# Banded attention and a PReLU feed-forward: the slots of the opening rearranged

## The chip, the core and the metric

The kernel runs on one core of a Trainium2 chip. The core has a matrix engine (PE, with its weight loads shown as PEld), a vector engine (DVE), a scalar engine (ACT), a general engine (POOL) and a queue that issues most of the DMAs (SP). Each works through its own instructions in the order in which they are written and waits where an operand is not ready. The metric is device time in microseconds (us); less is better.

## The reference

Inputs are `q`, `k`, `v` of shape (8, 8, 576, 64): batch, heads, positions, head size. Attention is causal with a window of 64 positions; its output, as 4608 tokens of 512 values, goes through a feed-forward layer of width 2048:

```python
rel = pos[:, None] - pos[None, :]
scores = np.where((rel >= 0) & (rel < 64), scale * q @ k.T, -1e9)
attn = softmax(scores);  x = attn @ v            # -> 4608 x 512
h = x @ w_in
g = np.maximum(h, 0) + alpha * np.minimum(h, 0)
out = (g @ w_out).astype(np.float32)
```

The weights come as 64-bit floats. The kernel keeps more precision than one reduced product would give: every operand of the two large products is a high part and a low part, and each product is three (low x high, high x low, high x high).

## The kernel before

**Tiles and blocks.** The 4608 tokens are 36 tiles of 128. They form blocks of 2, 2, 2 and then 3 tiles; `f` counts 16 slices of 128 of the hidden width. One *cell* (n, f) is block n with slice f: the hidden product H (L300, twelve matmuls into a PSUM bank `ph`); the slopes (L309, ACT: bank times a slope, into `g`); the larger (L310, DVE: maximum of the other slope and `g`); the split (L319, ACT, high part `gh`; L320, POOL, low part `gl`); and the output product (L332, three matmuls for each tile, accumulated over all 16 slices in a bank of their own).

**Attention of one tile.** Scores (L209, PE); per head a mask, row minimum and its readout (L223, DVE) and an exponential (L226, ACT); scaling by the reciprocal sum (L232 and L233 on DVE, L234 on POOL); transposes (L247, PE) with a copy (L248, ACT); values (L259, PE); the split of the result into `xh` (L262, ACT) and `xl` (L263, DVE). Its loads are L180, L183 and L191.

**Conversion of the weights.** DMAs bring the 64-bit weights as pairs of 32-bit words, in 32 *chunks*: chunk 2f is slice f of `w_in`, chunk 2f+1 that of `w_out`. A chunk c passes through: fetch (L114, SP); exponent mask `two` (L123, DVE) and its rebias (L125, ACT); mantissa mask `man` (L130, DVE) and its conversion (L133, ACT); the joins `exp` (L140, DVE) and `val` (L142, DVE); the product of both (L148, POOL); the high part (L159, ACT); the low part (L163, POOL), which needs the high part. H(n, f) needs chunk 2f, the output product of (n, f) needs chunk 2f+1.

**The opening.** `opening()` is written out by hand, and each engine runs it in this order. After a prologue with tiles 0 and 1 and chunks 0 to 2 it goes through *slots*, j = 3, 4, and so on. In slot j chunk j is masked, chunk j-1 joined and multiplied, chunk j-2 split. Slots also hold the cells of blocks 0 and 1 and one of five attention steps for tiles 2 to 5 (`STEPS`, slots 3 to 22: load, half the scores and their exponentials; the other half and a scaling; a scaling and half the transposes; the other half; the values). Block 0 has a cell in every second slot from slot 3 on, since a slice takes two chunks. Block 1 joins when tiles 2 and 3 are there, at slot 13; for five slots there are then two cells a slot to catch up, and after that one, of alternating blocks, until slot 34.

The order within a slot before is: H of the cell; high part (j-2); joins (j-1); fetch (j+2); low part (j-2); slopes and larger of the cell; product (j-1); exponent mask and rebias (j); split of the cell; mantissa mask and conversion (j); output product of an earlier cell; a second cell, whole; the attention step.

**Buffers that matter.** `ph` has two PSUM banks, shared by H and `two`; `psa` two, shared by `man`, the scores, the transposes and the values; `raw` holds three chunks; `val` and `exp` two each.

**After the opening** a loop over blocks 2 to 12 alternates cells with eighths of the attention of later tiles. Its instructions stand behind those of the opening on every engine. The diff does not touch it, but for `m_slopes`, cut in two and called one after the other.

Of the kernel before, what the change touches and what calls it, by code (L numbers as in the profile page):

```python
# [8 lines left out]
F32 = mybir.dt.float32  # L9
# [4 lines left out]
ALU = mybir.AluOpType  # L14
# [11 lines left out]
def banded_attention_then_prelu_ffn(  # L26
# [93 lines left out]
    def mask_exp(c):  # L120
        d = cv[c]
        d["two"] = two = ps_h.tile([P, E], I32, tag="ph", name=f"two_{c}")
        nc.vector.tensor_scalar(out=two, in0=d["high"], scalar1=0x7FF00000, scalar2=None,  # L123
                                op0=ALU.bitwise_and)
        nc.scalar.activation(two, two, AF.Relu, scale=8.0, bias=ebias)  # L125

    def mask_man(c):
        d = cv[c]
        d["man"] = man = ps_a.tile([P, E], I32, tag="psa", name=f"man_{c}")
        nc.vector.tensor_scalar(out=man, in0=d["high"], scalar1=0xFFFFF, scalar2=0x100000,  # L130
                                op0=ALU.bitwise_and, op1=ALU.bitwise_or)

        nc.scalar.activation(man.bitcast(F32), man, AF.Copy,  # L133
                             scale=s20_sb[:, c // 2:c // 2 + 1] if c % 2 else 2.0**-20)

    def join(c):
        d = cv[c]
        d["val"] = val = io.tile([P, E], F32, tag="val", name=f"val_{c}", bufs=2)
        d["exp"] = exp = io.tile([P, E], I32, tag="exp", name=f"exp_{c}", bufs=2)
        nc.vector.scalar_tensor_tensor(out=exp, in0=d["high"], scalar=-2**31, in1=d["two"],  # L140
                                       op0=ALU.bitwise_and, op1=ALU.bitwise_or)
        nc.vector.scalar_tensor_tensor(out=val, in0=d["low"],  # L142
                                       scalar=s52_sb[:, c // 2:c // 2 + 1] if c % 2 else 2.0**-52,
                                       in1=d["man"].bitcast(F32), op0=ALU.mult, op1=ALU.add)
# [54 lines left out]
    def a_score(t, halves=(0, 1)):  # L199


        d = st[t]
        q, k = d["q"], d["k"]
        d["s"] = [a_bank(t, f"s_{t}_{u}") for u in halves]
        for e in range(NP):
            for h in range(2):
                for u in halves:
                    r, out_ = slice(u * D, (u + 1) * D), slice(h * W, (h + 1) * W)
                    nc.tensor.matmul(d["s"][u - halves[0]][out_, e], q[r, e, h, :], k[r, e, :, h, :],  # L209
                                     start=True, stop=True)  # L210
# [17 lines left out]
    def a_norm(t, halves=(0, 1)):  # L228
        d = st[t]
        g = slice(halves[0] * NP, (halves[-1] + 1) * NP)  # L230
        w, rc = d["w"][:, g, :], d["rc"][:, g]
        nc.vector.tensor_scalar_add(rc, d["sm"][:, g], 1e-9)  # L232
        nc.vector.reciprocal(rc, rc)  # L233
        nc.gpsimd.tensor_tensor(out=w, in0=w, in1=rc.unsqueeze(2).broadcast_to(list(w.shape)),  # L234
                                op=ALU.mult)
# [69 lines left out]
    def m_slopes(n, f):  # L305
        nt = len(blocks[n]) * P
        ph = gs[n, f]
        g = gp.tile([P, nt], F32, tag="g", name=f"g_{n}_{f}", bufs=2)
        nc.scalar.activation(g, ph[:, :nt], AF.Copy, scale=sa_sb[:, f:f + 1])  # L309
        nc.vector.scalar_tensor_tensor(out=g, in0=ph[:, :nt], scalar=s_sb[:, f:f + 1], in1=g,  # L310
                                       op0=ALU.mult, op1=ALU.max)
        gs[n, f] = g

    def m_split(n, f):
        nt = len(blocks[n]) * P
        g = gs[n, f]
        gh = gp.tile([P, nt], F32R, tag="gh", name=f"gh_{n}_{f}")
        gl = gp.tile([P, nt], F32R, tag="gl", name=f"gl_{n}_{f}")
        nc.scalar.copy(gh, g)  # L319
        nc.gpsimd.tensor_tensor(out=gl, in0=g, in1=gh.bitcast(F32), op=ALU.subtract)  # L320
        gs[n, f] = gh, gl
# [27 lines left out]
    def cell(n, f):  # L349
        m_hidden(n, f)  # L350
        m_slopes(n, f)
        m_split(n, f)
        late.append((n, f))
        while len(late) > LAG:
            m_out(*late.pop(0))
# [3 lines left out]
    def soft(t, u):  # L359
        for e in range(NP):  # L360
            a_soft(t, u * NP + e)
# [15 lines left out]
    def opening():  # L377
        a_load(0)
        fetch(0)
        nc.scalar.dma_start(alpha_sb, alpha.rearrange("(f p) -> p f", p=P))  # L380
        a_load(1)
        v_load(0)
        fetch(1)
        v_load(1)
        fetch(2)
        a_score(0)
        soft(0, 0)
        soft(0, 1)
        mask_exp(0)
        mask_man(0)  # L390
        a_norm(0)
        nc.vector.tensor_scalar(out=s_sb, in0=alpha_sb, scalar1=1.0, scalar2=-2.0, op0=ALU.is_gt, op1=ALU.mult)
        nc.vector.tensor_scalar_add(s_sb, s_sb, 1.0)
        nc.vector.tensor_scalar_mul(s20_sb, s_sb, 2.0**-20)
        nc.vector.tensor_scalar_mul(s52_sb, s_sb, 2.0**-52)
        nc.vector.tensor_tensor(out=sa_sb, in0=s_sb, in1=alpha_sb, op=ALU.mult)
        join(0)
        fetch(3)
        product(0)
        a_score(1)  # L400
        a_transpose_pe(0, 0)
        a_transpose_pe(0, 1)
        high_part(0)
        soft(1, 0)
        soft(1, 1)
        a_value(0)
        low_part(0)
        mask_exp(1)
        mask_man(1)
        a_norm(1)  # L410
        load(2)
        join(1)
        fetch(4)
        product(1)
        mask_exp(2)
        mask_man(2)
        a_transpose_pe(1, 0)
        a_transpose_pe(1, 1)
        high_part(1)
        low_part(1)  # L420
        a_value(1)

        done, wait = [0, 0], []
        first = [0, 5 * sizes[1]]
        j = LEAD
        while done != [NF, NF] or wait:

            ready = [n for n in range(2) if j - LEAD >= first[n]]
            at = min(NF, (j - LEAD) // 2 + 1)
            behind = sum(at - done[n] for n in ready)  # L430
            cells = []
            for _ in range(min(behind, 2 if behind > 2 else 1)):
                n = min(ready, key=lambda n: done[n])
                cells.append((n, done[n]))
                done[n] += 1
            if cells:
                m_hidden(*cells[0])
            if 0 <= j - 2 < 2 * NF:
                high_part(j - 2)
            if j - 1 < 2 * NF:  # L440
                join(j - 1)
            fetch(j + 2)
            if j - 2 < 2 * NF:
                low_part(j - 2)
            if cells:
                m_slopes(*cells[0])
            if j - 1 < 2 * NF:
                product(j - 1)
            if j < 2 * NF:
                mask_exp(j)  # L450
            if cells:
                m_split(*cells[0])
            if j < 2 * NF:
                mask_man(j)
            if wait and 2 * wait[0][1] + 1 + LEAD <= j:
                m_out(*wait.pop(0))
            for c in cells[1:]:
                m_hidden(*c)
                m_slopes(*c)
                m_split(*c)  # L460
                if wait and 2 * wait[0][1] + 1 + LEAD <= j:
                    m_out(*wait.pop(0))
            wait += cells
            while len(wait) > 2:
                m_out(*wait.pop(0))
            t, k = divmod(j - LEAD, 5)
            if t + 2 < EARLY:
                STEPS[k](t + 2)
            j += 1
# [60 lines left out]
```

## Time and profile before

| | |
|---|---|
| time, median of 3 runs | 979.17 us (977.67 to 979.46) |
| profiled execution | 978.52 us, its span 976.8 us |
| PE busy | 927.3 us, 95% of the span |
| DVE busy | 464.1 us, 48% |
| ACT busy | 422.4 us, 43% |
| POOL busy | 350.9 us, 36% |
| chain that ended last | PE 86%, ACT 6%, DVE 3% |

Shares are of the whole span, and the opening is its first 183 us or so. Of the groups that only the opening has (conversion), POOL's product (32 of 1.285 us) and low part (33 of about 1.28 us) are the longest instructions. A row of the timeline gives the start, the length, the engine, the line, the operation, result and operands, and in brackets the idle time before it and what ended that.

### The profile page before, as it was taken

The page shows a single profiled execution, that of the slowest core. Times are in us where ns is not written, and L with a number is a line of the kernel's source. Part 1 is how long each engine was busy: PE and PEld are TensorE (multiplying, and loading weights), DVE is VectorE, ACT ScalarE, POOL GpSimd, SP SyncE. Part 2 cuts the span into 40 slices and gives each one's busy share as a digit, 9 for nine tenths or more (in the row PEclk, how much of TensorE's full clock was granted, in tenths as well). Part 3 has the DMA queues.
Part 4 walks back from the last instruction along what each step waited for, and adds up shares of the span by engine and source line. Part 5 has one row for each costly group of instructions (what it writes and reads, how often), then busy time and mean ns, then how long its engine had stood idle before and what let it go on. Part 6 is the DMA issues. An engine that isn't in the chain of part 4 may idle for free.

```text
span 976.8 us, 17281 instructions
## 1 busy us (share of the span) xinstructions
PE 927.3 (95%) x6576; PEld 814.7 (83%) x6576; DVE 464.1 (48%) x1394; ACT 422.4 (43%) x1174; POOL 350.9 (36%) x327
## 2 busy tenths in 40 slices
PE   3677988999999999999999999999999999999998
PEld 3556867888888888888888888889889889889997
DVE  4675678475444444444544454444444444441111
ACT  4565666644433442442443443433433433432322
POOL 3575689433223223223223322322232223222221
PEclk9879999999999999999999999999999999999999
DMA  9865384332321321321322322322322322100000
GB/s 212 176 164 140 98 197 138 106 79 59 89 66 30 98 61 36 90 66 41 87 61 48 87 55 55 87 55 54 87 56 54 87 56 55 55 1 1 33 1 33
DMA packets 96419, 74.54 MB, mean 76 GB/s; under 512 B 44624, under 2 KB 89680, under 8 KB 96336
## 3 DMA queue, kind: packets, MB, share of 16 engines
q1 hardware_dynamic: 94272, 73.42, 30.0%
q8 instruction: 52, 0.85, 0.4%
q10 hardware_dynamic: 2064, 0.01, 0.1%
q14 instruction: 31, 0.25, 0.1%
HBM read 63.97 MB, written 9.44 MB: 75 GB/s over the span
## 4 chain that ended last, share of the span: by engine, by line
PE 86%; ACT 6%; DVE 3%; issue 2%; DMA 1%; SPq 1%; POOL 1%; POOLq 0%; ACTq 0%
PE h L300 40%; PE o L332 38%; PE av L259 4%; PE s L209 4%; DVE two L123 1%; ACT two L125 1%; ACT w L226 1%; ACT g L309 1%; PE t L247 1%; ACT man L133 1%; SPq L183 1%; DMA q<-qT 1%; DMA v<-vN 1%; DVE pt L242 1%; ACT gh L319 1%
## 5 line engine op out<-in xcount | busy, mean ns | idle before, releaser
L320 POOL TENSOR_TENSOR gl<-g,gh 128x384 fp32r<-128x384 f32 (+1 forms) x208 | 197.2, 948 | 471.5 <-ACT gh L319 369.8
L310 DVE SCALAR_TENSOR_TENSOR g<-h,s_sb,g 128x384 f32<-128x384 f32 (+1 forms) x208 | 122.1, 587 | 301.8 <-ACT g L309 299.2
L332 PE MATMUL o<-wout_h,gl 128*128 128x512 f32 x576 | 227.9, 396 | 13.9 <-POOL gl L320 13.9
L332 PE MATMUL o<-wout_l,gh 128*128 128x512 f32 x576 | 228.4, 397 | 0.0
L332 PE MATMUL o<-wout_h,gh 128*128 128x512 f32 x576 | 226.0, 392 | 0.0
L309 ACT ACTIVATE g<-h,sa_sb 128x384 f32<-128x384 f32 (+1 forms) x208 | 115.6, 556 | 254.1 <-PE h L300 253.7
L300 PE MATMUL h<-xh,win_l 128*128 128x384 f32 (+1 forms) x832 | 180.7, 339 | 11.1 <-POOL win_l L163 5.9
L319 ACT CAST gh<-g 128x384 fp32r<-128x384 f32 (+1 forms) x208 | 101.1, 486 | 188.7 <-DVE g L310 188.6
L242 DVE STREAM_TRANSPOSE pt<-w 32x256 f32<-32x256 f32 x360 | 157.0, 436 | 53.5 <-POOL w L234 48.3
L300 PE MATMUL h<-xl,win_h 128*128 128x384 f32 (+1 forms) x832 | 170.3, 326 | 0.0
L300 PEld LDWEIGHTS h<-xh,win_l 128*128 128x128 f32 x832 | 139.3, 190 | 36.0 <-DVE g L310 8.4
L300 PE MATMUL h<-xh,win_h 128*128 128x384 f32 (+1 forms) x832 | 169.0, 324 | 0.0
L300 PEld LDWEIGHTS h<-xl,win_h 128*128 128x128 f32 x832 | 143.5, 190 | 0.3 <-DVE xl L263 0.2
L300 PEld LDWEIGHTS h<-xh,win_h 128*128 128x128 f32 x832 | 140.9, 190 | 0.0
L226 ACT ACTIVATE w<-w,nm 128x128 f32<-128x128 f32 x288 | 112.2, 392 | 54.7 <-DVE nm L223 54.7
L332 PEld LDWEIGHTS o<-wout_h,gl 128*128 128x128 f32 x576 | 108.8, 189 | 31.7 <-POOL gl L320 15.2
L332 PEld LDWEIGHTS o<-wout_h,gh 128*128 128x128 f32 x576 | 109.1, 189 | 24.3
L332 PEld LDWEIGHTS o<-wout_l,gh 128*128 128x128 f32 x576 | 109.2, 190 | 14.4
L234 POOL TENSOR_TENSOR w<-w,rc 128x1024 f32<-128x1024 f32 (+1 forms) x40 | 69.0, 1726 | 120.1 <-DVE rc L233 99.0
L223 DVE CUSTOM_DVE_ANT_0 w<-s,masks 128x128 f32<-128x128 f32 x288 | 64.2, 286 | 64.6 <-PE s L209 64.5
L209 PE MATMUL s<-k,q 64*64 64x128 f32 x1152 | 50.1, 287 | 12.0 <-DMA q<-qT 10.7
L209 PEld LDWEIGHTS s<-k,q 64*64 64x64 f32 x1152 | 38.9, 139 | 26.9 <-DMA k<-kT 11.8
(43 smaller groups left out, 509.8 us busy)
## 6 DMA issues: line engine op xcount, KB each, us to landing
k<-kT SPq DMA_DIRECT2D x72, 256.0 KB, 4.0
v<-vN SPq DMA_DIRECT2D x72, 256.0 KB, 4.2
q<-qT SPq DMA_DIRECT2D x144, 64.0 KB, 3.6
out<-os SPq DMA_DIRECT2D x36, 256.0 KB, 2.4
raw<-w_in SPq DMA_DIRECT2D x16, 512.0 KB, 4.3
raw<-w_out SPq DMA_DIRECT2D x16, 512.0 KB, 3.5
alpha_sb<-alpha ACTq DMA_DIRECT2D x1, 8.0 KB, 4.6
```

What stands on the lines that cost most here:

```text
L209: nc.tensor.matmul(d["s"][u - halves[0]][out_, e], q[r, e, h, :], k[r, e, :, h, :], start=True, stop=True)
L223: nc.vector.tensor_tensor_reduce(out=w, in0=d["s"][u % len(d["s"])][:, e], in1=mask, op0=ALU.add, op1=ALU.min, scale=-SCALE, scalar=3.0e38 ...
L226: nc.scalar.activation(w, w, AF.Exp, scale=-1.0, bias=nm, accum_out=d["sm"][:, g:g + 1])
L234: nc.gpsimd.tensor_tensor(out=w, in0=w, in1=rc.unsqueeze(2).broadcast_to(list(w.shape)), op=ALU.mult)
L242: nc.vector.transpose(pt[ks, :, r], w[r, :, ks])
L259: nc.tensor.matmul(av[r, e, u * W:(u + 1) * W], v[:, e, u, r], pt[:, u * NP + e, h * W:(h + 1) * W], start=True, stop=True)
L300: nc.tensor.matmul(ph[:, :nt], wt[:, c, fs], xt[:, c, xs], start=(k == 0), stop=(k == 3 * NP - 1))
L309: nc.scalar.activation(g, ph[:, :nt], AF.Copy, scale=sa_sb[:, f:f + 1])
L310: nc.vector.scalar_tensor_tensor(out=g, in0=ph[:, :nt], scalar=s_sb[:, f:f + 1], in1=g, op0=ALU.mult, op1=ALU.max)
L319: nc.scalar.copy(gh, g)
L320: nc.gpsimd.tensor_tensor(out=gl, in0=g, in1=gh.bitcast(F32), op=ALU.subtract)
L332: nc.tensor.matmul(po[t], gt[:, ts], wt[:, f, :], start=(f == 0 and k == 0), stop=(f == NF - 1 and k == 2))
```

## The change

The work stays the same, to the instruction; the order in the opening changes, and three helpers are cut in two so that their parts can stand apart.

- `mask_exp` gives its rebias to `rebias`; `join` becomes `join_exp` and `join_man`; `m_slopes` gives its second half to `m_larger`.
- A cell in three successive slots: its H is written at the end of a slot (ahead of the attention step), slopes, larger and split in the next slot, its output product at the head of the one after. A second cell's H stands at the head of its slot, the rest of it near the end.
- Conversion interleaved by chunk on DVE: `exp` (j-1), `two` (j), `val` (j-1), `man` (j), where it was `exp`, `val` (j-1), `two`, `man` (j).
- On ACT the order in a slot becomes slopes, high part, `gh`, rebias, mantissa conversion (it was high part, slopes, rebias, `gh`, mantissa conversion). On POOL it becomes low part, `gl`, product (it was low part, product, `gl`).
- The fetch of chunk j+2 stands behind the joins and the product of chunk j-1.
- `pick` replaces the choice of cells; slots 14 to 17 and 19 have two cells (it was 13 to 17).
- In the prologue tiles 0 and 1 are scaled and transposed by halves, the slope constants come first, and load(2) stands ahead of the second half of tile 0's transposes.

```diff
     def mask_exp(c):
...
+
+    def rebias(c):
+        two = cv[c]["two"]
         nc.scalar.activation(two, two, AF.Relu, scale=8.0, bias=ebias)
...
-    def join(c):
+    def join_exp(c):
...
+    def join_man(c):
...
         nc.scalar.activation(g, ph[:, :nt], AF.Copy, scale=sa_sb[:, f:f + 1])
+        gs[n, f] = ph, g
+
+    def m_larger(n, f):
+        nt = len(blocks[n]) * P
+        ph, g = gs[n, f]
         nc.vector.scalar_tensor_tensor(out=g, in0=ph[:, :nt], scalar=s_sb[:, f:f + 1], in1=g,
...
         a_score(0)
         soft(0, 0)
         soft(0, 1)
+        a_norm(0, (0,))
         mask_exp(0)
+        rebias(0)
         mask_man(0)
-        a_norm(0)
...
+        a_norm(0, (1,))
+        a_transpose_pe(0, 0)
+        a_score(1)
+        soft(1, 0)
+        join_exp(0)
+        join_man(0)
+        product(0)
         fetch(3)
-        product(0)
-        a_score(1)
-        a_transpose_pe(0, 0)
+        load(2)
         a_transpose_pe(0, 1)
+        soft(1, 1)
+        a_norm(1, (0,))
+        a_value(0)
         high_part(0)
-        soft(1, 0)
-        soft(1, 1)
-        a_value(0)
         low_part(0)
         mask_exp(1)
+        rebias(1)
+        a_transpose_pe(1, 0)
         mask_man(1)
-        a_norm(1)
-        load(2)
-        join(1)
+        a_norm(1, (1,))
+        join_exp(1)
+        join_man(1)
+        product(1)
         fetch(4)
-        product(1)
-        mask_exp(2)
-        mask_man(2)
-        a_transpose_pe(1, 0)
         a_transpose_pe(1, 1)
+        a_value(1)
         high_part(1)
         low_part(1)
-        a_value(1)
+        mask_exp(2)
+        rebias(2)
+        mask_man(2)
...
+        def pick(j):
+            ready = [n for n in range(2) if j >= first[n] and 2 * done[n] + 2 <= j and done[n] < NF]
+            if not ready:
+                return None
+            n = min(ready, key=lambda n: done[n])
+            done[n] += 1
+            return n, done[n] - 1
+
+        todo = pick(LEAD - 1)
+        m_hidden(*todo)
         j = LEAD
...
+            if more:
+                m_hidden(*more)
+            if wait and 2 * wait[0][1] + 4 <= j:
+                m_out(*wait.pop(0))
+            if todo:
+                m_slopes(*todo)
             if 0 <= j - 2 < 2 * NF:
                 high_part(j - 2)
             if j - 1 < 2 * NF:
-                join(j - 1)
-            fetch(j + 2)
-            if j - 2 < 2 * NF:
+                join_exp(j - 1)
+            if todo:
+                m_larger(*todo)
+            if 0 <= j - 2 < 2 * NF:
                 low_part(j - 2)
...
             if j < 2 * NF:
                 mask_exp(j)
-            if cells:
-                m_split(*cells[0])
+            if todo:
+                m_split(*todo)
+                wait.append(todo)
+            if j < 2 * NF:
+                rebias(j)
+            if j - 1 < 2 * NF:
+                join_man(j - 1)
+                product(j - 1)
+            fetch(j + 2)
             if j < 2 * NF:
                 mask_man(j)
...
+            if more:
+                m_slopes(*more)
+                m_larger(*more)
+                m_split(*more)
+                if wait and 2 * wait[0][1] + 4 <= j:
                     m_out(*wait.pop(0))
-            wait += cells
+                wait.append(more)
+            todo = pick(j)
+            if todo:
+                m_hidden(*todo)
             while len(wait) > 2:
                 m_out(*wait.pop(0))
             t, k = divmod(j - LEAD, 5)
```

The last lines of the loop, which start the attention step of tile t+2, are unchanged and stand behind this.

More of the change, by code (lines that the diff above doesn't have):

```diff
@@ L134, in mask_man @@
                              scale=s20_sb[:, c // 2:c // 2 + 1] if c % 2 else 2.0**-20)
-    def join(c):
+    def join_exp(c):
         d = cv[c]
-        d["val"] = val = io.tile([P, E], F32, tag="val", name=f"val_{c}", bufs=2)
         d["exp"] = exp = io.tile([P, E], I32, tag="exp", name=f"exp_{c}", bufs=2)
@@ L141, in join @@
                                        op0=ALU.bitwise_and, op1=ALU.bitwise_or)
+    def join_man(c):
+        d = cv[c]
+        d["val"] = val = io.tile([P, E], F32, tag="val", name=f"val_{c}", bufs=2)
         nc.vector.scalar_tensor_tensor(out=val, in0=d["low"],
@@ L351, in cell @@
         m_slopes(n, f)
+        m_larger(n, f)
         m_split(n, f)
@@ L385, in opening @@
         fetch(2)
+        nc.vector.tensor_scalar(out=s_sb, in0=alpha_sb, scalar1=1.0, scalar2=-2.0, op0=ALU.is_gt, op1=ALU.mult)
+        nc.vector.tensor_scalar_add(s_sb, s_sb, 1.0)
+        nc.vector.tensor_tensor(out=sa_sb, in0=s_sb, in1=alpha_sb, op=ALU.mult)
+        nc.vector.tensor_scalar_mul(s20_sb, s_sb, 2.0**-20)
+        nc.vector.tensor_scalar_mul(s52_sb, s_sb, 2.0**-52)
         a_score(0)
@@ L388, in opening @@
         soft(0, 1)
+        a_norm(0, (0,))
         mask_exp(0)
+        rebias(0)
         mask_man(0)
-        a_norm(0)
[L392 to L397, printed above, removed]
+        a_norm(0, (1,))
@@ L409, in opening @@
         mask_man(1)
-        a_norm(1)
-        load(2)
-        join(1)
+        a_norm(1, (1,))
+        join_exp(1)
+        join_man(1)
+        product(1)
         fetch(4)
-        product(1)
-        mask_exp(2)
-        mask_man(2)
-        a_transpose_pe(1, 0)
         a_transpose_pe(1, 1)
+        a_value(1)
         high_part(1)
         low_part(1)
-        a_value(1)
-        done, wait = [0, 0], []
-        first = [0, 5 * sizes[1]]
-        j = LEAD
[L426 to L435, printed above, removed]
-            if cells:
-                m_hidden(*cells[0])
+        mask_exp(2)
@@ new lines, in opening @@
+        rebias(2)
+        mask_man(2)
+        done = [0, 0]
+        first = [0, LEAD + 5 * sizes[1]]
+        todo = None
+        wait = []
+        def pick(j):
[7 more added lines that the diff above has]
+        m_hidden(*todo)
+        j = LEAD
@@ L438, in opening @@
+        while todo or wait or j < 2 * NF + 2:
+            at = min(NF, (j - 1) // 2)
+            more = None
+            if sum(at - done[n] for n in range(2) if j >= first[n]) > 1:
+                more = pick(j - 1)
+            if more:
[4 more added lines that the diff above has]
+                m_slopes(*todo)
             if 0 <= j - 2 < 2 * NF:
@@ L440, in opening @@
             if j - 1 < 2 * NF:
-                join(j - 1)
-            fetch(j + 2)
-            if j - 2 < 2 * NF:
+                join_exp(j - 1)
+            if todo:
+                m_larger(*todo)
+            if 0 <= j - 2 < 2 * NF:
                 low_part(j - 2)
[L445 to L448, printed above, removed]
             if j < 2 * NF:
                 mask_exp(j)
-            if cells:
-                m_split(*cells[0])
+            if todo:
[7 more added lines that the diff above has]
+            fetch(j + 2)
             if j < 2 * NF:
                 mask_man(j)
[L455 to L461, printed above, removed]
+            if more:
[3 more added lines that the diff above has]
+                if wait and 2 * wait[0][1] + 4 <= j:
                     m_out(*wait.pop(0))
-            wait += cells
+                wait.append(more)
+            todo = pick(j)
+            if todo:
+                m_hidden(*todo)
             while len(wait) > 2:
```

## The prediction

> **What bounds the kernel now.** I read the busy time by stretch first. All but the opening is PE alone; in the opening no engine is full.
>
> ```profile
> 60.00:90.00 30.00, 21.04 (x162) 17.58 (x163) 21.22 (x58) 19.18 (x52) 18.95 (x18) 0.83 0.71 173
> 150.00:180.00 30.00, 26.44 (x160) 21.65 (x159) 21.46 (x36) 18.84 (x40) 26.14 (x25) 1.00 0.26 84
> 230.00:300.00 70.00, 70.00 (x517) 62.21 (x516) 37.46 (x119) 28.45 (x85) 20.93 (x19) 1.00 0.26 65
> ```
>
> Columns: length, busy time of PE, PE weight loads, DVE, ACT, POOL, PE clock, DMA share, GB/s. From 230 us PE is busy without a break, so the diff's stretch, up to about 183 us, is worth its own length and no more; what follows is shifted. Before 183 us four engines are each busy for two thirds to nine tenths: chains of waits set the slot, not a load.
>
> The pace of the slots is read from the timeline of DVE, at the larger-step (L310) of the first cell in slots 3, 13, 20, 23 and 31:
>
> ```profile
> 35.84 0.48 DVE L310 SCALAR_TENSOR_TENSOR g<-h,s_sb,g 128x256 f32<-128x256 f32 x1 [1.61 <-ACT g L309]
> 84.60 0.48 DVE L310 SCALAR_TENSOR_TENSOR g<-h,s_sb,g 128x256 f32<-128x256 f32 x1 [0.63 <-ACT g L309]
> 128.25 0.48 DVE L310 SCALAR_TENSOR_TENSOR g<-h,s_sb,g 128x256 f32<-128x256 f32 x1 [0.73 <-ACT g L309]
> 141.31 0.48 DVE L310 SCALAR_TENSOR_TENSOR g<-h,s_sb,g 128x256 f32<-128x256 f32 x1
> 169.86 0.48 DVE L310 SCALAR_TENSOR_TENSOR g<-h,s_sb,g 128x256 f32<-128x256 f32 x1
> ```
>
> So the stages take 48.8 us (slots 3 to 12, a cell in every second slot, five in all), 43.7 (13 to 19), 13.1 (20 to 22) and 28.6 (23 to 30, eight slots of 3.57). Both orders give each of these stages the same number of cells and chunks; I compare them stage by stage.
>
> **The late slots (23 to 30).** One slot of before, on POOL, DVE and ACT, and the end of the conversions, where hi (L159) waits for the product (L148) in the open:
>
> ```profile
> 155.25 1.29 POOL L163 TENSOR_TENSOR wout_l<-val,wout_h 128x512 fp32r<-128x512 f32 x1 [0.28 <-ACT wout_h L159]
> 156.51 1.29 POOL L148 TENSOR_TENSOR val<-val,exp 128x512 f32<-128x512 f32 x1
> 157.77 0.74 POOL L320 TENSOR_TENSOR gl<-g,gh 128x256 fp32r<-128x256 f32 x1
> 158.86 1.27 POOL L163 TENSOR_TENSOR win_l<-val,win_h 128x512 fp32r<-128x512 f32 x1 [0.35 <-ACT win_h L159]
> ...
> 155.99 0.69 DVE L123 TENSOR_SCALAR two<-raw 128x512 int32<-128x512 int32 x1
> 156.71 0.66 ACT L125 ACTIVATE two<-two,ebias 128x512 int32<-128x512 int32 x1 [1.15 <-DVE two L123]
> 157.29 0.40 ACT L319 CAST gh<-g 128x256 fp32r<-128x256 f32 x1
> 157.59 0.66 ACT L133 ACTIVATE man<-man,s_sb 128x512 f32<-128x512 int32 x1
> 158.17 0.62 ACT L159 CAST win_h<-val 128x512 fp32r<-128x512 f32 x1
> 158.68 0.48 ACT L309 ACTIVATE g<-h,sa_sb 128x256 f32<-128x256 f32 x1
> ...
> 174.36 1.29 POOL L148 TENSOR_TENSOR val<-val,exp 128x512 f32<-128x512 f32 x1
> 175.68 0.62 ACT L159 CAST wout_h<-val 128x512 fp32r<-128x512 f32 x1 [1.29 <-POOL val L148]
> 176.38 1.31 POOL L163 TENSOR_TENSOR wout_l<-val,wout_h 128x512 fp32r<-128x512 f32 x1
> ```
>
> Before, POOL does low part, product, gl. While it does gl (0.74), ACT turns the fresh product into the next high part; POOL waits only 0.28 to 0.35 for it. After, the order is low part, gl, product: the next instruction on POOL is the low part that needs hi, and hi needs the product that has just ended. From the last three rows this handover costs 0.03 + 0.62 + 0.08 = 0.73 with nothing on POOL beneath it. The new POOL cycle is low 1.26 (start to start) + gl 0.74 + product 1.29 + 0.73 = 4.02, called 4.0, against 3.57. The masks and joins, interleaved, need less on DVE and ACT: slopes 0.48, larger 0.48, three passes of DVE like the mask's 0.69 and the conversion's 0.66 in a row are at most 3.7, inside 4.0. Eight slots at +0.43: **+3.4 us**. Bounds: -2.2, if the handover is hidden (1.26 + 0.74 + 1.29 = 3.29 a slot), and +4. I take the upper side because no instruction stands between.
>
> **The slots with attention steps.** An output product now comes one slot after its split, but the hidden product H moved to the end of a slot and stands ahead of the attention step on PE, and the next slot's slopes stand behind that step's work on ACT. Before, H headed the slot and ran beneath the step's work. Costs, in the order of the chain of waits, first at the low clock, then at the full one, and the mask-and-minimum of the scores from the groups:
>
> ```profile
> 41.21 1.90 PE s L209 x16
> 43.11 2.88 PE h L300 x12
> 52.24 0.85 PE t L247 x4
> 62.08 1.55 ACT w L226 x8
> 94.69 1.04 PE s L209 x16
> 102.28 0.44 PE t L247 x4
> 105.53 1.46 PE h L300 x12
> 106.99 1.37 PE o L332 x6
> 114.45 1.10 PE av L259 x32
> 115.57 0.59 ACT xh L262
> L223 DVE CUSTOM_DVE_ANT_0 w<-s,masks 128x128 f32<-128x128 f32 x288 | 64.2, 286 | 64.6 <-PE s L209 64.5
> ```
>
> The tail between H and the next slopes is score, minimum, four exponentials: 1.04 + 0.29 + 1.55 = 2.9 (3.7 at the low clock); or transposes and their copy (0.59, as xh): 1.0 (1.4); or values and xh: 1.7.
>
> Slots 13 to 19: in a slot with two cells the path is slopes 0.48, hi with its handover 0.70, low 1.26, gl 0.74 and 0.08 to PE, output product 1.37, H 1.46: 6.1, plus the tail. One with a single cell is slopes, larger (0.48 each), H 1.46, tail. In order: 13 single with scores 5.3, 14 with scores 9.0, 15 and 16 with transposes 7.1 each, 17 with values 7.8, 18 single with scores 5.3, 19 with scores 9.0: 50.6 against 43.7, **+7.0**. Bounds: 0, if ACT's step work finds room elsewhere, and +9. Slots 20 to 22 are single, at 4.0 by the POOL cycle, since their transposes and values fit inside it: 12.0 against 13.1, **-1.1**.
>
> Slots 3 to 12: here block 0 alone has cells and H(0,f) needs the low part of chunk 2f, made in H's own slot. From slopes to slopes, over two slots: slopes 0.48, hi 0.70, low 1.26, gl 0.74, product 1.32, hi 0.70, low 1.34 = 6.5; then H, then the tail of slots 4 (scores), 6 (transposes), 8 (scores), 10 (transposes), 12 (values); and some 2 us for the exponentials of slots 3 and 9 that stand ahead of hi on ACT (0 to 3.1, twice 1.55). At the full clock 5 x 7.96 + 5.8 + 2.0 + 1.7 + 2 = 51.3; at the low one 5 x 9.38 + 7.4 + 2.8 + 1.7 + 2 = 60.8. Which clock? Before it flips:
>
> ```profile
> 67.49 0.79 PE L332 MATMUL o<-wout_h,gl 128*128 128x512 f32 x1 [2.68 <-POOL gl L320]
> 64.00:68.00 4.00, 1.32 (x17) 0.84 1.23 189
> 68.00:72.00 4.00, 4.00 (x15) 0.50 1.09 287
> ```
>
> After an idle stretch of 2.68 us PE runs at 0.50. In the new order PE idles from the end of the tail to the next output product, which comes 3.2 us after the slopes: 0.6 to 1.8 + 3.2 less the odd slot's own PE work, 2.6 to 4.1 us. By the row three of the four bring the low clock; I take two thirds of the way, 57.6: **+8.8**, bounds +2.5 and +12.
>
> The Trainium skill, page "TensorE: Matmul & The Clock Gate", section "Part 1: The HAM clock gate", has the clock fall only after an idle window of about 3.4 us, which one of these four gaps fills; by it the early stage would be about 53 us, and the whole 4 us less than I forecast. The trace disagrees with its figure, since 2.68 us were enough.
>
> **The prologue.** Before, the path to the first slopes is, from the chain of waits:
>
> ```profile
> 14.15 2.22 PE s L209 x28
> 19.40 3.08 ACT w L226 x16
> 25.33 1.91 POOL w L234
> 27.28 1.98 PE t L247 x8
> 35.34 0.48 ACT g L309
> ```
>
> Scaling and transposing tile 1 by halves takes half of 1.91 and half of 1.98 off it, 1.95. Its exponentials could start at 16.7 rather than 19.40; the copies and the joins of chunk 0 put between them give about 1.1 of this 2.7 back. **-3.5**, bounds -2 and -4.7. The five slope constants move to DVE's idle time before 9.9 us. Loads keep their order on SP's queue but for load(2) and the fetches: a fetch now follows the joins, still a slot and a half, some 6 us, ahead of its first mask. I cost this at nothing; cover gone, each such slot would be late by what is missing.
>
> The end (slots 31 on): gl of the last two cells follows the last low part as before; 0.
>
> **Sum.** -3.5 + 8.8 + 7.0 - 1.1 + 3.4 = +14.6. The profiled execution took 978.52 (span 976.8), 0.65 below the median of 979.17; so 993.1 as a profiled execution, and 993.5 against the median.
>
> **The rivals.** (1) PE keeps its full clock in slots 3 to 12: the sum is +8.3, 987. For it speaks that the steps' own products break up the gaps; against it the 0.50 above. (2) The half clock reaches the late slots too: output product and H then take 5.6 (twice 1.37 and 1.46), 1.6 more than 4.0 in 11 slots, +18 on top, 1011. Against: gaps there are 1.2 us, and the clock of before in 150 to 180 us is 1.00. (3) No change: the tails do not hold the slopes up, because ACT waits for something else at that time anyway. Then slots 13 to 19 stay at 43.7 and the early ones end at their lower bound: -3.5 + 2.5 - 1.1 + 3.4 = +1.3, 980. Against: ACT works in order, and the new chain is longer than the old. (4) Faster: the split's gh now stands ahead of the rebias on ACT, which before made it wait for a mask on DVE and the rebias (0.69 + 0.58 from the start of L123 at 155.99 to that of L319 at 157.29). If the cell's own path sets the early pairs, five of them gain 1.3 each, 6.4, the late slots fall to POOL's load (-2.2), and the prologue gives 3.5: -12, 967. It decides where the product-to-hi-to-low handover lies beneath other work of POOL, under about 0.3 us of waiting for hi as before; the order low, gl, product leaves it bare.
>
> **How the numbers follow.** The forecast has 0.60, (1) 0.20, (2) 0.04, (3) 0.06, (4) 0.10. Differences under 0.2%, 2 us, can't be told from none. Slower: 0.60 + 0.20 + 0.04 = 0.84; same 0.06; faster 0.10. The range goes from rival (1) with the upper prologue bound and the tails partly hidden, 982, to the upper bounds of early and middle stage less some of the late one, 1002; outside it lie (2), (3) and (4), 0.20.
>
> **What would show it.** Right: in the late slots POOL's low part idles about 0.7 us for hi in each, and the larger-steps stand 4.0 apart; first slopes near 31.8 us; in slots 5, 9, 14, 15 the slopes start right behind exponentials or the copy of the transposes; PE's clock near 0.5 in much of 35 to 85 us. Wrong: late slots at 3.3 or less, or slopes that start at H's end in the attention slots, or PE without gaps from 90 to 130 us; then (3) or (4) holds. A fetch landing after its mask is due would be a cost that I left at nothing.

## The result and the profile after

| | before | after |
|---|---|---|
| time, median of 4 runs each | 978.42 us (975.58 to 979.46) | 1006.13 us (1004.24 to 1008.29) |
| ratio | 1 | 1.0291 (95%: 1.0274 to 1.0307) |
| profiled execution, span | 978.52, 976.8 us | 1004.24, 1002.2 us |

The change costs 27.7 us between the medians. The profiled execution of after is the fastest of its four runs, so the trace holds 25.4 us of this (1002.2 - 976.8) and the other 2 are spread among runs.

From the page of after: TensorE's row in the 40 slices (25.06 us each) and, from the costliest groups, the first product of H with the waits ahead of it; then that last row for before.

```profile
PE   4666878799999999999999999999999999999998
...
L306 PE MATMUL h<-xh,win_l 128*128 128x384 f32 (+1 forms) x832 | 181.7, 341 | 25.4 <-POOL win_l L169 14.6
```

```profile
L300 PE MATMUL h<-xh,win_l 128*128 128x384 f32 (+1 forms) x832 | 180.7, 339 | 11.1 <-POOL win_l L163 5.9
```

PE is full from the ninth slice on; the loss lies in the first eight. The H rows say where: the idle time ahead of H's first matmuls grows from 11.1 to 25.4 us, and what the low part of a `w_in` chunk ends of it from 5.9 to 14.6. Not all of the loss is idle time: over the whole span PE is idle for 65.5 us (1002.2 - 936.7) against 49.5 (976.8 - 927.3), and busy for 9.4 us longer with the same 6576 matmuls.

The pace, from the timeline: the first slopes on ACT, then DVE's larger-steps (now L321) at slots 3, 13, 20, 23 and 31.

```profile
32.31 0.47 ACT L315 ACTIVATE g<-h,sa_sb 128x256 f32<-128x256 f32 x1 [0.48 <-PE h L306]
...
32.81 0.48 DVE L321 SCALAR_TENSOR_TENSOR g<-h,s_sb,g 128x256 f32<-128x256 f32 x1 [0.71 <-ACT g L315]
...
91.26 0.48 DVE L321 SCALAR_TENSOR_TENSOR g<-h,s_sb,g 128x256 f32<-128x256 f32 x1
...
146.73 0.48 DVE L321 SCALAR_TENSOR_TENSOR g<-h,s_sb,g 128x256 f32<-128x256 f32 x1 [0.58 <-ACT g L315]
...
163.77 0.48 DVE L321 SCALAR_TENSOR_TENSOR g<-h,s_sb,g 128x256 f32<-128x256 f32 x1
...
195.83 0.48 DVE L321 SCALAR_TENSOR_TENSOR g<-h,s_sb,g 128x256 f32<-128x256 f32 x1 [1.84 <-ACT g L315]
```

Stage by stage, from these starts and those of before:

| stage | before | after | difference | forecast |
|---|---|---|---|---|
| up to slot 3 | 35.8 | 32.8 | -3.0 | -3.5 |
| slots 3 to 12 | 48.8 | 58.5 | +9.7 | +8.8 |
| slots 13 to 19 | 43.7 | 55.5 | +11.8 | +7.0 |
| slots 20 to 22 | 13.1 | 17.0 | +4.0 | -1.1 |
| slots 23 to 30 | 28.6 | 32.1 | +3.5 | +3.4 |
| the rest of the span | | | -0.6 | 0 |

Three terms are within 1 us of the forecast; two are short by 5 each.

**A late slot.** POOL's and ACT's rows in the order of their starts:

```profile
171.90 1.30 POOL L169 TENSOR_TENSOR wout_l<-val,wout_h 128x512 fp32r<-128x512 f32 x1 [0.96 <-ACT wout_h L165]
173.16 0.74 POOL L331 TENSOR_TENSOR gl<-g,gh 128x256 fp32r<-128x256 f32 x1
173.85 1.29 POOL L154 TENSOR_TENSOR val<-val,exp 128x512 f32<-128x512 f32 x1
175.17 0.62 ACT L165 CAST win_h<-val 128x512 fp32r<-128x512 f32 x1 [0.46 <-POOL val L154]
175.87 1.27 POOL L169 TENSOR_TENSOR win_l<-val,win_h 128x512 fp32r<-128x512 f32 x1 [0.73 <-ACT win_h L165]
```

Low part to low part takes 3.97, and 0.73 of it POOL stands still for the high part: product to high part to low part lies bare, as forecast. In every second slot POOL waits longer, 0.96 in the first row, and the low parts stand 4.19 apart: there the high part stands behind the slopes on ACT (slopes at 170.84, high part at 171.21), and these slopes wait for H. A pair of slots takes 8.16.

**The slots with attention steps.** PE and ACT around the start of slot 15, and in slots 20 and 21, in the order of their starts:

```profile
103.52 1.09 PE L215 MATMUL s<-k,q 64*64 64x128 f32 x16
...
105.00 0.40 ACT L232 ACTIVATE w<-w,nm 128x128 f32<-128x128 f32 x1 [3.51 <-DVE nm L229]
...
106.52 0.74 PE L306 MATMUL h<-xh,win_l 128*128 128x256 f32 x4 [1.90 <-DVE exp L142]
106.55 0.46 ACT L315 ACTIVATE g<-h,sa_sb 128x256 f32<-128x256 f32 x1
...
148.62 1.22 PE L306 MATMUL h<-xh,win_l 128*128 128x256 f32 x4 [2.72 <-POOL win_l L169]
...
150.49 1.05 PE L306 MATMUL h<-xh,win_h 128*128 128x256 f32 x4
151.34 0.89 PE L253 MATMUL t<-ident,w 128*128 128x128 f32 x4
...
152.26 0.59 ACT L254 COPY pt<-t 128x512 f32<-128x512 f32 x1 [2.52 <-PE t L253]
152.75 0.48 ACT L315 ACTIVATE g<-h,sa_sb 128x256 f32<-128x256 f32 x1
```

The rows from 148.62 on are the mechanism in one view. H waits 2.72 us for the low part of its own slot; the transposes stand behind H on PE, their copy behind them, and the next slopes behind the copy on ACT. H's last matmuls end at 151.54, and the slopes start 1.2 us later. In slot 15 it is the exponentials that stand there: the slopes start at 106.55, right behind them.

Length, busy time of PE and its matmul records, clock, DMA share and GB/s (the columns between are left out by choosing PE's alone) in three stretches of after (the second is slots 13 to 19), then the first two of them for before:

```profile
36.00:88.00 52.00, 34.60 (x185) 0.64 0.60 150
...
91.26:146.73 55.47, 45.97 (x320) 0.94 0.49 118
...
148.00:152.00 4.00, 3.38 (x17) 0.57 0.58 158
```

```profile
36.00:88.00 52.00, 35.60 (x258) 0.80 0.66 166
...
84.60:128.25 43.65, 40.90 (x318) 1.00 0.59 138
```

So slots 13 to 19 have PE busy for 5.1 us longer at the lower clock and idle for 6.7 us more (9.5 against 2.8). The same count gives 4.4 us of longer busy time in slots 3 to 12 (37.45 against 33.05, at 0.68 and 0.79) and 2.2 in 20 to 22 (13.08 against 10.87, at 0.90 and 1.00). In the late slots the clock is 1.00 in both.

### The profile page after: what moved, and what is told of

The parts are those of the page before. It is cut to its first block, busy times and chain, and to the rows that moved or that the text cites. A ratio compares the mean times of both kernels' runs of the same rounds, so it can differ in the third digit from the quotient of the medians.

```text
span 1002.2 us, 17280 instructions
## 1 busy us (share of the span) xinstructions
PE 936.7 (93%) x6576; PEld 820.6 (82%) x6576; DVE 461.6 (46%) x1398; ACT 426.9 (43%) x1174; POOL 350.8 (35%) x329
## 4 chain that ended last, share of the span: by engine, by line
PE 83%; POOL 7%; issue 4%; DVE 3%; ACT 2%; DMA 0%; SPq 0%; POOLq 0%; DVEq 0%; ACTq 0%
PE h L306 39%; PE o L343 36%; PE s L215 4%; PE av L265 4%; POOL val L154 2%; POOL win_l L169 2%; POOL gl L331 1%; POOL wout_l L169 1%; ACT w L232 1%; POOL w L240 1%; DVE pt L248 1%; DVE w L229 0%; DVE g L321 0%; DMA q<-qT 0%; PE t L253 0%
## 5 line engine op out<-in xcount | busy, mean ns | idle before, releaser
L321 DVE SCALAR_TENSOR_TENSOR g<-h,s_sb,g 128x384 f32<-128x384 f32 (+1 forms) x208 | 122.1, 587 | 321.7 <-ACT g L315 320.1
L343 PE MATMUL o<-wout_h,gl 128*128 128x512 f32 x576 | 231.2, 401 | 4.0 <-POOL gl L331 4.0
L306 PE MATMUL h<-xh,win_l 128*128 128x384 f32 (+1 forms) x832 | 181.7, 341 | 25.4 <-POOL win_l L169 14.6
L215 PEld LDWEIGHTS s<-k,q 64*64 64x64 f32 x1152 | 38.0, 138 | 27.0 <-PE o L343 11.1
```

What stands on the lines that cost most here:

```text
L306: nc.tensor.matmul(ph[:, :nt], wt[:, c, fs], xt[:, c, xs], start=(k == 0), stop=(k == 3 * NP - 1))
L343: nc.tensor.matmul(po[t], gt[:, ts], wt[:, f, :], start=(f == 0 and k == 0), stop=(f == NF - 1 and k == 2))
```

## The experiments

Every kernel is compared by the starts of the exponent masks (L123), which all of them have once in each slot. Times are medians; "before" was run beside each on the same chip: 978.48 beside step first, the POOL order, both of these and the prologue; 977.01 beside `gl` first, block 0 later, three edits and the filler; 978.23 beside the other four. All stages come from one profiled execution of each kernel. In the expectations A is the bare handover on POOL, B the attention step between H and the slopes, D the clock, E the wait of the second H for the exponent join.

| kernel | us | ratio (95%) | 3 to 12 | 13 to 19 | 20 to 22 | 23 to 30 |
|---|---|---|---|---|---|---|
| before | | 1 | 48.8 | 43.7 | 13.1 | 28.6 |
| after | 1006.1 | 1.0291 (1.0274-1.0307) | 58.4 | 55.5 | 17.0 | 32.1 |
| step first | 982.1 | 1.0050 (1.0032-1.0067) | 47.6 | 47.7 | 14.1 | 32.6 |
| POOL order | 1006.9 | 1.0305 (1.0284-1.0327) | 58.2 | 60.6 | 16.5 | 30.4 |
| both of these | 990.7 | 1.0135 (1.0118-1.0152) | 51.9 | 53.6 | 14.3 | 30.4 |
| before, `gl` first | 998.1 | 1.0227 (1.0193-1.0262) | 49.0 | 44.2 | 15.7 | 41.7 |
| block 0 later | 998.3 | 1.0224 (1.0196-1.0252) | 48.9 | 60.7 | 16.4 | 32.0 |
| both blocks later | 997.3 | 1.0192 (1.0165-1.0220) | 50.1 | 56.4 | 13.1 | 29.5 |
| the same, POOL order late | 997.0 | 1.0184 (1.0158-1.0210) | 53.1 | 56.6 | 14.1 | 30.0 |
| three edits | 981.9 | 1.0046 (1.0029-1.0063) | 48.1 | 51.2 | 14.2 | 30.4 |
| early join | 1004.1 | 1.0251 (1.0223-1.0280) | 61.7 | 56.9 | 15.9 | 32.4 |
| filler | 998.5 | 1.0220 (1.0202-1.0238) | 53.7 | 55.4 | 16.4 | 32.0 |
| prologue alone | 974.6 | 0.9968 (0.9958-0.9978) | 49.2 | 44.9 | 13.1 | 28.6 |
| prologue and filler | 975.7 | 0.9973 (0.9961-0.9986) | 49.9 | 43.7 | 13.1 | 28.6 |

**Step first.** After, with the attention step ahead of the next cell's H; nothing else moves.

```diff
+            t, k = divmod(j - LEAD, 5)
+            if t + 2 < EARLY:
+                STEPS[k](t + 2)
             todo = pick(j)
             if todo:
                 m_hidden(*todo)
             while len(wait) > 2:
                 m_out(*wait.pop(0))
-            t, k = divmod(j - LEAD, 5)
-            if t + 2 < EARLY:
-                STEPS[k](t + 2)
```

> The changed kernel with one move: the attention step of a slot stands ahead of the hidden product that closes the slot, not behind it. Theory B (the step's work on PE and ACT between H and the next slopes is what the slots 3 to 22 lose): from the larger-step of slot 3 to that of slot 23, 131.0 us in the changed kernel and 105.5 in the one before, it takes 112 to 120; total 10 to 20 us under the changed kernel. Rival (the half clock of PE and the wait of H for its own slot's low part alone): the stage stays within 4 us of 131. Both: slots 23 to 31 stay at 4.0.

24.0 of the 27.7 us go: 10.8 in slots 3 to 12, 7.8 in 13 to 19, 2.9 in 20 to 22, 1.3 ahead of slot 3's mask, nothing in the late ones, which have no step. PE and ACT at the start of slot 14:

```profile
80.92 1.09 PE L215 MATMUL s<-k,q 64*64 64x128 f32 x16 [2.32 <-issue]
81.94 0.74 PE L306 MATMUL h<-xh,win_l 128*128 128x256 f32 x4
...
83.56 0.39 ACT L232 ACTIVATE w<-w,nm 128x128 f32<-128x128 f32 x1
...
84.42 0.47 ACT L315 ACTIVATE g<-h,sa_sb 128x256 f32<-128x256 f32 x1 [0.39 <-PE h L306]
```

Now scores come first, and the exponentials run beneath H; the slopes wait 0.39 for H itself and no longer behind exponentials. This one order is the main cause.

**POOL order.** After, with `gl` cut off the split and put behind the product.

```diff
                 product(j - 1)
+            if todo:
+                m_low(*todo)     # the GpSimd subtraction that m_split held
             fetch(j + 2)
```

> The changed kernel with one exchange on POOL: in a slot the low part, then the product, then gl, as before the change; all else as changed. Theory A (the bare handover from product to high part to low part sets the late slots): the larger-steps of slots 23 to 31, 4.01 us apart in the changed kernel, come at 3.3 to 3.6, so that stage takes 27 to 29 us instead of 32.1; early pairs lose some 0.7 each; total 4 to 9 us under the changed kernel. Rival (the late slots wait for H, whose weights are made in its own slot, and for what follows it): they stay at 3.9 to 4.1 and the total within 2 us of the changed kernel.

The late slots go from 4.01 to 3.80, a third to a half of the way to the 3.57 of before or the 3.29 of POOL's load, and between what the theory and its rival expected. Slots 13 to 19 lose 5.2, and the whole gains nothing: PE's waits for `gl` there rise from 1.9 to 4.5 us in all, which is half of the loss; the rest is not traced. What a late slot waits for now, from PE, POOL and ACT:

```profile
175.88 1.30 POOL L169 TENSOR_TENSOR wout_l<-val,wout_h 128x512 fp32r<-128x512 f32 x1 [0.96 <-ACT wout_h L165]
...
179.16 0.51 PE L347 MATMUL o<-wout_h,gl 128*128 128x512 f32 x1 [1.08 <-POOL gl L335]
179.28 1.30 POOL L169 TENSOR_TENSOR win_l<-val,win_h 128x512 fp32r<-128x512 f32 x1 [0.17 <-ACT win_h L165]
...
180.66 0.71 PE L306 MATMUL h<-xh,win_l 128*128 128x256 f32 x4
...
182.43 0.48 ACT L315 ACTIVATE g<-h,sa_sb 128x256 f32<-128x256 f32 x1 [0.75 <-PE h L306]
```

In every second slot POOL waits 0.17 where it waited 0.73, so there the handover is hidden; in the others it still waits 0.96 for a high part that stands behind the slopes. Every second H needs the low part of its own slot (it ends at 180.58, H starts at 180.66), and the slopes behind it are late. Steps of 3.40 and 4.20 alternate. **Both of these** edits together:

> Both edits on the changed kernel: POOL in the order low part, product, gl, and the attention step ahead of the closing hidden product. If the two losses are separate, the gains add: 15 to 27 us under the changed kernel, 980 to 992. If one hides the other, it equals the better of the two alone within 3 us. Under 978 would mean that the three-slot cell gains by itself, once these two are out of its way.

The order of POOL keeps its late gain (30.4) and costs 4.3 in slots 3 to 12 and 5.9 in 13 to 19 on top of step first.

**Before, `gl` first.** The slots of before, with the product behind the first cell's split.

```diff
-            if j - 1 < 2 * NF:
-                product(j - 1)
             if j < 2 * NF:
                 mask_exp(j)
             if cells:
                 m_split(*cells[0])
+            if j - 1 < 2 * NF:
+                product(j - 1)
```

> The kernel before with one exchange on POOL: in a slot the low part, then gl of the first cell, then the product, as in the changed kernel; all else as before. Theory A (product, high part and low part in a row with nothing of POOL beneath): the late slots, 3.57 us apart, come at 3.9 to 4.2, so slots 23 to 31 take 31 to 34 us instead of 28.6, with 0.7 us of POOL's idle time before every low part; total 3 to 8 us over the kernel before. Rival (the loss of the late slots needs the cell's new places too): within 1.5 us of the kernel before.

The late slots go to 5.21, against 3.57 before and far over the 3.9 to 4.2 expected: the same exchange costs more here than in after. POOL and ACT of one slot:

```profile
149.13 0.62 ACT L159 CAST win_h<-val 128x512 fp32r<-128x512 f32 x1 [1.53 <-POOL val L148]
149.65 0.47 ACT L309 ACTIVATE g<-h,sa_sb 128x256 f32<-128x256 f32 x1
...
151.27 0.66 ACT L125 ACTIVATE two<-two,ebias 128x512 int32<-128x512 int32 x1 [1.15 <-DVE two L123]
151.86 0.40 ACT L319 CAST gh<-g 128x256 fp32r<-128x256 f32 x1
...
152.33 0.74 POOL L320 TENSOR_TENSOR gl<-g,gh 128x256 fp32r<-128x256 f32 x1 [1.24 <-ACT gh L319]
153.03 1.28 POOL L148 TENSOR_TENSOR val<-val,exp 128x512 f32<-128x512 f32 x1
...
154.34 0.62 ACT L159 CAST wout_h<-val 128x512 fp32r<-128x512 f32 x1 [1.60 <-POOL val L148]
```

High part, slopes, larger and mask on DVE, rebias, `gh`, `gl`, product, and the next high part: one chain with no gap, round the whole slot (149.13 to 154.34). So `gl` ahead of the product is dear where `gh` comes late; in after `gh` stands ahead of the rebias, and the handover is what is left bare.

**Block 0 later, both blocks later.** After, with a cell's H a slot later, so that it never needs the low part of its own slot; first for block 0 alone, then for both, which takes one slot more at the end.

```diff
-            ready = [... 2 * done[n] + 2 <= j ...]
+            ready = [... 2 * done[n] + 2 + (n == 0) <= j ...]   # block 0 later
+            ready = [... 2 * done[n] + 3 <= j ...]              # both blocks later
```

> The changed kernel with block 0's cells picked one slot later: a hidden product no longer needs the low part that is made in its own slot; the end comes no later, since the two blocks only exchange places. Theory C (that wait, with the attention step behind it, makes the slots 3 to 12 and 20, 22 long): slots 3 to 13 in 46 to 53 us instead of 58.5, slots 20 to 22 in 12 to 14 instead of 17.0; total 8 to 18 us under the changed kernel. Rival (the attention step behind H alone): the total falls by less than 4, as the step still stands between H and the slopes. Late slots 3.9 to 4.1 by theory A, since POOL's order is untouched.

Slots 3 to 12 fall from 58.4 to 48.9, the time of before, with the step still behind H. So the early loss needs both: an H that waits for its own slot's low part, and a step behind it; taking away either is enough. Slots 13 to 19 grow by 5.2, since six of them now have two cells instead of five. From slot 20 on the blocks only change places, and block 1 has the wait; for those slots the second kernel is needed:

> The changed kernel with the cells of both blocks picked one slot later, so that no hidden product needs a low part of its own slot, at the price of one slot at the end. Theory C: slots 3 to 13 by the exponent masks in 46 to 51 us instead of 58.4 and slots 20 to 22 in 12 to 14.5 instead of 17.0. Theory A: the late slots still stand 4.0 apart, now evenly, where they alternated 3.4 and 4.75, since POOL's product, high part and low part remain in a row; 8.0 to 8.1 a pair against 8.16. Rival to A (H's wait alone sets them): 3.4 to 3.6. Total 6 to 14 us under the changed kernel.

Slots 20 to 22 are at 13.1, the time of before, against 17.0. In the late slots the masks stand 3.4 apart at first and 4.0 at the end; POOL's low parts are 4.0 to 4.2 apart from the first of them on, so the 29.5 of the table is not POOL's pace. POOL at the end:

```profile
171.08 1.29 POOL L169 TENSOR_TENSOR win_l<-val,win_h 128x512 fp32r<-128x512 f32 x1 [0.73 <-ACT win_h L165]
172.33 0.73 POOL L331 TENSOR_TENSOR gl<-g,gh 128x256 fp32r<-128x256 f32 x1
173.01 1.30 POOL L154 TENSOR_TENSOR val<-val,exp 128x512 f32<-128x512 f32 x1
175.04 1.29 POOL L169 TENSOR_TENSOR wout_l<-val,wout_h 128x512 fp32r<-128x512 f32 x1 [0.73 <-ACT wout_h L165]
```

Each slot is low part, `gl`, product and a wait of 0.73, with no other wait: 3.96. This is the forecast's cycle of 4.0, alone. **The same with the POOL order** low part, product, `gl` from slot 20 on:

> The same, and from slot 20 on POOL in the order low part, product, gl. Theory A: without H's wait for its own slot's low part the exchange now gives its whole 0.6 a slot: 3.3 to 3.5 apart instead of 4.0, 27 us for slots 23 to 31 against 32.1 in the changed kernel and 28.6 before. Rival (a third chain at 4.0, of PE or ACT): 3.8 or more. Total 3 to 6 us under the kernel with both blocks later.

It settles at 3.77, not at POOL's load: steps of 3.48 and 4.05 alternate. What is waited for, from PE and ACT:

```profile
166.69 0.50 PE L347 MATMUL o<-wout_h,gl 128*128 128x512 f32 x1 [0.97 <-POOL gl L335]
...
169.86 0.47 ACT L315 ACTIVATE g<-h,sa_sb 128x256 f32<-128x256 f32 x1 [0.59 <-PE h L306]
```

The output product waits for `gl`, H stands behind it, and the slopes wait for H. So the bare handover sets 4.0, and with the POOL order a slot takes 3.80 with H's wait for its own low part and 3.77 without it. The two are so close that this wait is not shown to be what holds the POOL order at 3.80.

**Three edits.** After with step first, block 0 later, and the POOL order from slot 20 on.

> The changed kernel with three edits: the attention step ahead of the closing hidden product, block 0's cells a slot later, and from slot 20 on POOL in the order low part, product, gl. If theories A, B and C hold and their gains add: late slots 3.3 to 3.6 apart, slots 3 to 13 in 44 to 48 us, and a total of 965 to 976, under the kernel before. If block 0's wait was already hidden by moving the step: 979 to 982, as with the step alone, less 2 us of the late slots.

No better than step first alone, so the gains do not add: 2.3 won in the late slots, 3.5 lost in slots 13 to 19.

**Early join.** What is left in slots 13 to 19? In the rows of after the second H waits 1.90 us for `exp` (L142): it takes the PSUM bank of `two`, which the join frees, and the join stands behind the row minimums on DVE. Here the join moves to the end of its own slot, ahead of the step.

```diff
+        join_exp(2)
...
-            if j - 1 < 2 * NF:
-                join_exp(j - 1)
...
                 m_out(*wait.pop(0))
+            if j < 2 * NF:
+                join_exp(j)
```

> The changed kernel with one DVE instruction moved: the exponent join of a chunk stands at the end of its own slot, ahead of the attention step, and not at the head of the next. In slots with two cells the second hidden product needs the bank that this join sets free, and in the changed kernel it waits 1.6 to 1.9 us for it, behind the step's row minimums. Theory E (this wait is what slots 13 to 19 lost beyond the tails that were forecast, 55.5 against 50.6): they take 49 to 53 us; total 2 to 6 us under the changed kernel. Rival (PE reaches those products early and waits later, for gl): within 1 us of 55.5. Late slots stay at 4.0 to 4.1.

Slots 13 to 19 take 56.9, against 55.5, in the profiled execution, which is the slowest of the four (1007.87, their median 1004.06). PE no longer waits for the join, 5.3 us in three waits before the edit, but its waits for `gl` rise from 1.9 to 5.8: it reaches the output product sooner and waits there instead,

```profile
113.07 0.80 PE L343 MATMUL o<-wout_h,gl 128*128 128x512 f32 x1 [2.00 <-POOL gl L331]
```

2.00 us for `gl` in this row. So E falls as far as this one trace shows. Why slots 3 to 12 are 3.3 longer as well stays open.

**Filler.** After, with sixteen matmuls of 256 columns at the end of each slot from 3 to 12, into a bank that nothing reads; the output is the same.

```diff
+            if j < 13:
+                if j == LEAD:
+                    warm = ps_o.tile([P, E], F32, tag="po", name="warm")
+                for i in range(16):
+                    nc.tensor.matmul(warm[:, :2 * P], win_h[:, i % NP, :P], xh[:, i % NP, :2 * P],
+                                     start=True, stop=True)
             j += 1
```

> The changed kernel with 16 more matmuls of 256 columns at the end of each of the slots 3 to 12, into a PSUM bank that nothing reads; they are only there to keep PE busy in its idle stretches, and the output is untouched. Theory D (PE's half clock makes part of the early stage's loss): the granted clock from 36 to 88 us, 0.5 to 0.7 for the most part, rises to 0.85 or more, and slots 3 to 13 take 51 to 55 us instead of 58.5; total 3 to 7 us under the changed kernel. Rival (the chain waits for ACT and POOL, and PE's speed is hidden): 57 to 61 us at whatever clock.

The same columns as above, for the filler, for the prologue alone, and for the prologue with the filler:

```profile
36.00:88.00 52.00, 44.69 (x385) 0.97 0.61 147
```

```profile
36.00:88.00 52.00, 38.27 (x259) 0.72 0.70 168
```

```profile
36.00:88.00 52.00, 46.92 (x415) 1.00 0.69 165
```

The clock goes from 0.64 to 0.97, slots 3 to 12 from 58.4 to 53.7, and the whole is 7.6 us shorter (6.9 by the two ratios to before). So D holds in after: raising the clock takes 4.7 us off the early stage, about the 4.4 us that PE was busy longer there, and the other 4.9 (53.7 - 48.8) stay at nearly the full one. The 4.7 is a net gain, since the fillers take PE's time too.

**Prologue alone.** The slots of before with the prologue of after.

> The kernel before with the prologue of the changed one alone; its slots are as before. Theory: first slopes at about 32.3 us instead of 35.34, and the whole 2 to 3.5 us under the kernel before. Rival (given back, since the early slots wait for conversions or loads that do not come sooner): the same total within 1 us, with longer slots 3 to 8.

3.9 us faster than before, and faster than both kernels: 974.59 (973.76 to 976.55). All slot stages but 13 to 19 (+1.2) are within 0.5 us of before. **With the filler:**

> The kernel before with the changed kernel's prologue (974.6 by itself) and with 16 more matmuls into an unread PSUM bank at the end of each of the slots 3 to 12, the output untouched. Theory D: the kernel before, too, loses time to the half clock there (0.80 granted from 36 to 88 us, with H 2.9 and output product 2.4 to 2.8 at the low rate): the clock rises above 0.9 and slots 3 to 13 take 43 to 47 us instead of 49.2; total 969 to 973. Rival (the slots of before wait on ACT and DVE while PE is slow): 974 to 976; or the fillers stand in front of output products and it gets slower, 976 to 980.

975.73: the clock goes from 0.72 to 1.00, and nothing is gained. That does not show the half clock to be hidden in the slots of before, for there the fillers stand right ahead of the next H. PE and ACT of this kernel, around the start of slot 5:

```profile
40.31 2.18 PE L488 MATMUL warm<-xh,win_h 128*128 128x256 f32 x16
42.33 0.64 PE L306 MATMUL h<-xh,win_l 128*128 128x256 f32 x4
...
43.97 0.47 ACT L315 ACTIVATE g<-h,sa_sb 128x256 f32<-128x256 f32 x1 [1.04 <-PE h L306]
```

H follows the fillers without a gap, and the slopes wait 1.04 for H where they waited 0.35 without the fillers. The next four H of block 0 start in the same way. What the clock gives, the fillers may take back; the two are not told apart.

## Why the prediction was wrong

The sign, the place and the main mechanism (the attention step between H and the slopes, the bare handover on POOL) were right. The size was not: 993.5 forecast, 982 to 1002 as range, 1006.1 measured. One step left out a wait, in slots 20 to 22, and one term was too small, that of slots 13 to 19.

- **Prologue, -3.5:** right. -3.0 in the trace; 3.9 us as a change of its own. The first slopes are at 32.31 (forecast 31.8).
- **Late slots, +3.4 by a POOL cycle of 4.02:** right in mechanism; the larger-steps are 4.01 apart. The bare handover is 0.73 in the trace as in the forecast, and alone it gives 3.96 (both blocks later). That the size fits so well is in part luck: POOL's slots of 3.97 and 4.19 make 4.08 on average, the 0.24 more in every second one being a wait through H that the forecast did not have, and two short steps at the start of the stage (3.39 and 4.19) hide it. The forecast also did not see that at almost the same length other chains wait: with the order reversed a slot is still 3.80, so that edit does not reach the lower bound of 3.29.
- **Slots 3 to 12, +8.8:** right in size (+9.7) and in cause, as step first (-10.8) and block 0 later (-9.5) show. Its two parts were off: the clock is worth 4.7, net, by the filler, where the forecast took two thirds of 9.5, and the time near the full clock is 53.7 where it had 51.3. The two errors nearly cancel, which is luck. Rival (1), full clock, falls by the 0.64.
- **Slots 20 to 22, -1.1:** the step that failed. "Their transposes and values fit inside it" took the slot for one of POOL's cycle alone. The forecast itself had said for slots 3 to 12 that H(0, f) needs the low part made in its own slot, and did not ask the same here. In slot 20 H starts 2.72 us late for that reason, runs at the half clock (its first group takes 1.22, against 0.74), and the copy stands between it and the slopes: slots of 6.5, 4.0 and 6.5 instead of three of 4.0. Without the wait the stage is at 13.1 (both blocks later), and with the step ahead at 14.1 (step first). Of the 4.0 us that the stage grew, 2.2 are PE busy longer at the lower clock. This term accounts for 5.1 of the shortfall.
- **Slots 13 to 19, +7.0:** the cause was right (step first takes 7.8 of the 11.8), the term mis-sized by 4.9. By larger-steps the slots took 5.7, 10.1, 8.4, 7.3, 9.1, 5.7 and 9.3, against 5.3, 9.0, 7.1, 7.1, 7.8, 5.3 and 9.0. The path was summed at the full clock, and the trace has 0.94 over the stage, with PE busy for 5.1 us longer than before; and it had no wait of the second H for its bank, which the trace shows (5.3 us in all). Removing that wait moved it elsewhere, so it is not shown to cost anything. The 5.1 us are about the size of the 4.9, but not all of PE's work is on the path, and no run here raised the clock in this stage alone: how the 4.9 divide between clock and waits stays open. Step first still has 4.1 us there over before; PE is busy for 2.9 of them (43.80 against 40.90, clock 0.96) and idle for 1.2, and what holds it is open too.
- **Rivals (2), (3) and (4):** all fall. The clock is 1.00 in the late slots of after; the tails hold the slopes (step first); and the handover is bare. The fetches, costed at nothing, cost nothing: from 32 to 200 us DVE has no wait for a DMA in after.
- **The range** reached 1002, from upper bounds of early and middle stage; the terms as they stand, with these two bounds, give 999 (-3.5 + 12 + 9 - 1.1 + 3.4 = 19.8 over 979.17), and the forecast against the median is 993.8 by its own sum, not 993.5. The bounds of the stage of slots 20 to 22 had no upper side at all: "fit inside" was taken as certain.

## What to carry to other kernels

Where an engine works in order, write down for each product which instruction it waits for, then ask what stands behind it on its own engine and on the next one: work written behind a product that waits is late by the whole wait, and so is all that follows that work. A rule found for one stage (here: this product needs a part made in its own slot) has to be asked again in every other stage. Moving the step ahead of the product cost one exchange of lines and gave back 24 of 28 us. With it the new slots are still 7.5 us slower than the old ones behind the same prologue (982.1 against 974.6): no run here shows a gain from the new order of the slots.

## What the runs showed of the hardware

**The length of the last idle stretch alone does not say whether the clock falls.** PE's rows of after, behind an idle stretch of 2.40 us, and behind the one of 1.90 us that ends at 106.52:

```profile
91.79 0.74 PE L306 MATMUL h<-xh,win_l 128*128 128x256 f32 x4 [2.40 <-DVE g L321]
...
107.09 0.68 PE L306 MATMUL h<-xl,win_h 128*128 128x256 f32 x4
107.57 1.05 PE L306 MATMUL h<-xh,win_h 128*128 128x256 f32 x4
```

Behind the 1.90 us, equal groups of four take 0.68 and then 1.05: the clock falls about 3 us after PE's work ended at 104.61 (103.52 + 1.09), when PE has been at work again for 1 us. Behind the stretch of 2.72 us the first group is already slow (1.22). But behind the 2.40 us the first group takes 0.74 and the next two 0.64 each, and the clock is 1.00 from 92 to 94 us; in before, too, a stretch of 2.42 us that ends at 58.06 left it at 1.00, and one of 2.68 us, ending at 67.49, did not. What besides the last stretch counts, the runs do not tell. The Trainium skill, page "TensorE: Matmul & The Clock Gate", section "Part 1: The HAM clock gate", has the clock fall after an idle window of about 3.4 us; the trace disagrees, since the three stretches ahead of a low clock, of 1.90, 2.68 and 2.72 us, are all shorter.

**Matmuls that nobody needs raise the clock, and cost PE's time.** Sixteen a slot took it to 0.97 and 1.00; the first saved 7.6 us, the second none, where the next H stood right behind them.
